# Memory scores over 40 key columns without a mask, with the spread moved into the normalisation

## The chip, the cores and the metric

The kernel runs on one core of a Trainium2 chip. The metric is the device time of one execution in microseconds (us); lower is better. A profile is one execution taken by the hardware profiler; its span runs from the first to the last instruction. Engines: PE is the matmul side of TensorE and PEld its weight loads, DVE is VectorE, ACT is ScalarE, POOL is GpSimd, SP is SyncE, which here issues DMAs.

## The reference

A layer of recurrent-memory attention followed by a squared-ReLU feed-forward block, on 2048 tokens of width 640, with 32 heads of 128 columns, 8 memory rows and segments of 32 tokens. The 64 segments depend on each other through the memory:

```python
idx = jnp.arange(L)                       # L = M + seg_len = 40
mask = (idx[:, None] < M) | (idx[:, None] >= idx[None, :])
mem = mem0
for s in range(n_seg):                    # 64 segments
    h = jnp.concatenate([mem, layernorm(x)[segment s]], axis=1)
    q, k, v = h @ Wq, h @ Wk, h @ Wv      # per head
    scores = where(mask, q @ k.T * Dh ** -0.5, -1e9)
    o = (softmax(scores) @ v) @ Wo
    mem = o[:, :M]                        # the next segment's memory
    outs.append(o[:, M:])
h = x + concatenate(outs)
out = h + relu(layernorm(h) @ w1 + b1) ** 2 @ w2 + b2
```

The mask lets the 8 memory queries see all 40 keys; token queries see the memory and the tokens up to their own.

## The kernel before

**Steps.** `step(b, sp)` is one segment s = 4b + sp (`NS` = 64 of them, in blocks of four). The matrix products of one row block are split over the four column groups of TensorE, so that four matmuls with 32 weight columns run at a time ("a round"). Of the 32 rows that a step projects itself, 8 are memory and 24 (`HD`) are tokens; the last 8 tokens of a segment (`TL`), the tail, are projected ahead for four segments at once (`tail_units`) and copied into place by `tails_in` (L320): queries to `qT` columns 32 to 39, keys to `kT`. `NK` = 40, `SEG` = 32.

**Memory queries.** The 8 memory queries of the 32 heads are worked on apart from the token queries, since only they are needed for the next step's memory. Heads come in two halves (n = 0, 1), four column groups g and four places j. `spread` (L369) copies the memory queries of head p into `qz[:, p, 8j:8j+8]`, with zeros elsewhere, so that four heads (j = 0 to 3) can accumulate into one 32-row block of PSUM, each in its own 8 rows. `scores(n)` (L413) makes 16 such matmuls at L421; before them, four matmuls at L416 put `bmask` into columns 32 to 63. The tail's 8 keys lie four times in `kT`, in columns 32 + 8j + k, and `bmask` is 0 where the column's j is the row's own and -1e9 elsewhere. `soft1(n)` (L425) takes the maximum (L427, DVE) and the exponential with its row sum (L430, ACT); `soft2(n)` (L434) the reciprocal (L436), the scaling to probabilities (L438) and a transpose of 32x32 blocks (L440), all on DVE. The copy in place j is what lets `values(n)` (L443) use the tail's values of four heads, stacked over (j, k) in `vt4`, in one matmul of 32 rows (L454), behind 16 for the other keys (L449).

**Token queries.** `token_scores` (L486) has a mask round at L489 and matmuls over 40 columns at L493; their softmax (L527 to L552) goes on beside the output product, and their values (`token_values`, L348) are made a step later. There the spread to four places is made with `same`, a 0/1 pattern (128 x 4 x 8) that is 1 where j is the row's own place: GpSimd multiplies the transposed tail probabilities by it at L572.

**Order.** All engines' queues are in the order of the program text; nothing is reordered by a scheduler. In a step TensorE has: query and key projections (L206), `scores(0)`, part of the value projection, `token_scores(0)`, more of the value projection, `scores(1)`, `token_scores(1)`, `token_values` of the step before (L355, L360), `values(0)`, the rest of the value projection, the output product (L238) with `values(1)` inside it, filling work (`fill`: tail projections and the tails' output products), and `mem_to_hT` (L312), which sets the new memory rows in the next step's input. The last step has no memory queries, so there are 63 x 2 calls of `scores`. `sm`, `pw` and `pm` share one PSUM buffer (`chn`, one buffer), so each waits until the one before has been read.

Of the kernel before, what the change touches and what calls it, by code (L numbers as in the profile page):

```python
# [8 lines left out]
ACT = mybir.ActivationFunctionType  # L9
ALU = mybir.AluOpType  # L10
AX = mybir.AxisListType
F32 = mybir.dt.float32
BF16 = mybir.dt.bfloat16
# [3 lines left out]
def kernel(  # L17
# [16 lines left out]
    nc = tc.nc  # L34
    _, S, D = A_x.shape
    _, H, E = A_Wq.shape
    M = A_mem0.shape[1]
    SEG = 32
    G = 4
# [8 lines left out]
    TL = SEG - HD  # L48
    NK = SEG + M
# [4 lines left out]
    scale = float(E) ** -0.5  # L54
    EPS = 1e-5
    NEG = -1.0e9
# [4 lines left out]
    const = ctx.enter_context(tc.tile_pool(name="const", bufs=1))  # L61
# [7 lines left out]
    s2 = ctx.enter_context(tc.tile_pool(name="s2", bufs=2))  # L69
# [8 lines left out]
    ident = const.tile([128, 128], BF16)  # L78
# [7 lines left out]
    nc.vector.memset(mask[:], 0.0)  # L86
    nc.gpsimd.affine_select(out=mask[0:32], in_=mask[0:32], compare_op=ALU.is_ge, fill=NEG, base=0,
                            pattern=[[0, HG], [-1, SEG]], channel_multiplier=1)
    bmask = const.tile([128, 4, TL], BF16)
    qz = const.tile([128, H, 32], BF16)  # L90
    nc.vector.memset(qz[:], 0.0)
    qzf = qz[:].rearrange("p h r -> p (h r)")
# [1 line left out]
    same = const.tile([128, 4, TL], BF16)  # L94
# [2 lines left out]
        nc.vector.tensor_copy(out=same[r], in_=ident[r, r].rearrange("p (j k) -> p j k", k=TL))  # L97
    nc.vector.tensor_reduce(out=diag[:], in_=same[:], op=ALU.add, axis=AX.X)
    nc.vector.tensor_copy(out=same[:], in_=diag[:].unsqueeze(2).to_broadcast([128, 4, TL]))
    nc.vector.tensor_scalar(out=bmask[:], in0=same[:], scalar1=-1.0, scalar2=-NEG, op0=ALU.add, op1=ALU.mult)  # L100
    qT = const.tile([128, H, NK], BF16)
    kT = const.tile([128, H, 2 * SEG], BF16)
    oT = const.tile([128, H, NK], BF16)
    nc.vector.memset(oT[:], 0.0)
    oTts = [const.tile([128, H, 32], BF16, name="oTt%d" % k) for k in range(2)]
# [30 lines left out]
    for ch in range(2):  # L136
        nc.scalar.dma_start(out=o0[32 * ch:32 * ch + M, :].rearrange("m (c f) -> m c f", f=64),
                            in_=A_mem0[0].rearrange("m (c t f) -> t m c f", t=2, f=64)[ch])
# [181 lines left out]
    def tails_in(b, sp, which="qk", h0=0, h1=H):  # L320
        q, k = [tails[b][w][:].rearrange("p h (k s) -> p h s k", s=4)[:, h0:h1, sp, :] if w in which else None for w in "qk"]
        if "q" in which:
            nc.gpsimd.tensor_copy(out=qT[:, h0:h1, SEG:NK], in_=q)
        if "k" in which:
            nc.gpsimd.tensor_copy(out=kT[:, h0:h1, SEG:2 * SEG].rearrange("p h (j k) -> p h j k", k=TL),  # L325
                                  in_=k.unsqueeze(2).to_broadcast([128, h1 - h0, 4, TL]))

    vt4s, stores = {}, []
    vt_d = dram.tile([NB, 4, 128, 2 * E], BF16)
# [50 lines left out]
    def step(b, sp, v=None):  # L380
# [30 lines left out]
        sms, ems, zms = {}, {}, {}  # L411

        def scores(n):  # L413
            sm = chn.tile([128, 512], F32, tag="ch", name="sm")
            for g in range(G):
                nc.tensor.matmul(sm[32 * g:32 * g + 32, SEG:2 * SEG], lhsT=ident[:, 0:32],  # L416
                                 rhs=bmask[:].rearrange("p j k -> p (j k)"), start=True, stop=False, skip_group_check=True)
            for j in range(4):
                for g in range(G):
                    p = n * 16 + g * 4 + j  # L420
                    nc.tensor.matmul(sm[32 * g:32 * g + 32, 0:2 * SEG], lhsT=qz[:, p, :], rhs=kT[:, p, :],  # L421
                                     start=False, stop=(j == 3), skip_group_check=True)
            sms[n] = sm

        def soft1(n):  # L425
            mx = s2.tile([128, 1], F32, tag="mx", name="mx")
            nc.vector.tensor_reduce(out=mx[:], in_=sms[n][:, 0:2 * SEG], op=ALU.max, axis=AX.X, negate=True)  # L427
            em = s2.tile([128, 2 * SEG], BF16, tag="em", name="em")
            zm = s2.tile([128, 1], F32, tag="zm", name="zm")
            nc.scalar.activation(out=em[:], in_=sms[n][:, 0:2 * SEG], func=ACT.Exp, bias=mx[:, 0:1], scale=1.0,  # L430
                                 accum_out=zm[:])
            ems[n], zms[n] = em, zm

        def soft2(n):  # L434
            rm = s2.tile([128, 1], F32, tag="rm", name="rm")
            nc.vector.reciprocal(out=rm[:], in_=zms[n][:])  # L436
            pm = s2.tile([128, 2 * SEG], BF16, tag="pmem", name="pmem")
            nc.vector.tensor_scalar(out=pm[:], in0=ems[n][:], scalar1=rm[:, 0:1], scalar2=None, op0=ALU.mult)  # L438
            pT = s2.tile([128, 2 * SEG], BF16, tag="pTm", name="pTm")
            nc.vector.transpose(out=pT[:], in_=pm[:])  # L440
            return pT
# [31 lines left out]
        def first_half():  # L473
            if not last:
                scores(0)
                soft1(0)
# [26 lines left out]
        if not last:  # L503
            pT0 = soft2(0)
# [3 lines left out]
        if not last:  # L508
            scores(1)
        token_scores(1)  # L510
        if not last:
            soft1(1)
# [11 lines left out]
        if not last:  # L524
            pT1 = soft2(1)
# [8 lines left out]
        if not last:  # L534
# [14 lines left out]
                                op=ALU.mult)  # L549
        pk = s1.tile([128, HG, 32], BF16, tag="pk", name="pk")  # L550
        nc.gpsimd.tensor_tensor(out=pk[:], in0=ek[:, :, 0:SEG], in1=rk[:].unsqueeze(2).to_broadcast([128, HG, SEG]),
                                op=ALU.mult)  # L552
# [9 lines left out]
        if not last:  # L562
            run(fill, 4 if outs else 6)
            mem_to_hT(o, hT4s[(s + 1) // 4], (s + 1) % 4)
            tails_in((s + 1) // 4, (s + 1) % 4)
# [5 lines left out]
        for u in range(2):  # L571
            nc.gpsimd.tensor_tensor(out=pTx[:, u], in0=pTt[:, u, HD:32].unsqueeze(1).to_broadcast([128, 4, TL]),  # L572
                                    in1=same[:], op=ALU.mult)
# [95 lines left out]
    def start():  # L669
# [5 lines left out]
        def stream(which, w, dst):  # L675
            pa = pop.tile([128, 4, 512], F32, tag="po", name="pa")
            for c in range(DC):
                for n in range(2):
                    proj(w, "half" if which == "v" else "columns", main, n, pa[:, n, :], c, c + 1)
                for n in range(2):  # L680
                    proj(w, "order" if which == "v" else "columns", lambda c: tail_rows(0, c), n, pa[:, 2 + n, :], c, c + 1)
                if c < DC - 1:
                    run(units, DC)
            for n in range(2):
                if which == "v":
                    nc.scalar.copy(out=v[:, n * 512:(n + 1) * 512], in_=pa[:, n, :])
                else:
                    row = rowtile()[:]
                    evac_row(which, row, pa[:, n, :])
                    flip(row, dst, n)  # L690
                    tail_out(0, which, n, pa[:, 2 + n, :])
                    run(late, 100)
                    tails_in(0, 0, which, n * 16, (n + 1) * 16)
            if which == "v":
                for n in range(2):
                    tail_out(0, which, n, pa[:, 2 + n, :])
# [110 lines left out]
    for t in range(S // NT):  # L807
# [6 lines left out]
        for fc in range(FC):  # L814
            ps = mmtile()
            for c in range(DC):
                if fc < FFULL:
                    nc.tensor.matmul(ps[:], lhsT=w1[:, c, fc * 128:(fc + 1) * 128], rhs=hnT[:, c, :],  # L818
                                     start=(c == 0), stop=(c == DC - 1))
                    continue  # L820
                for hh in range(2):
                    nc.tensor.matmul(ps[FREM * hh:FREM * (hh + 1), 0:HT], lhsT=w1[:, c, fc * 128:F],
                                     rhs=hnT[:, c, HT * hh:HT * (hh + 1)], start=(c == 0), stop=(c == DC - 1))
# [4 lines left out]
            if more and fc >= 1 and (fc - 1) // 3 < NK4:  # L828
                k, stage = divmod(fc - 1, 3)
# [10 lines left out]
        for q in range(NK4):  # L840
# [6 lines left out]
            for hh in range(2):  # L847
                k = pr + 2 * hh
                for fc in range(FFULL):
                    nc.tensor.matmul(y[:, hh, 0:DH], lhsT=f1T[:, fc, k * 128:(k + 1) * 128], rhs=w2[:, fc, cs],  # L850
                                     start=(fc == 0), stop=False, skip_group_check=True)
                if more and q and (hh == 0 or q == 1):
                    k = q if hh == 0 and q > 1 else hh
                    prep_pe(t + 1, k, hn_[k])()
            for hh in range(2):
                r = slice(FREM * hh, FREM * (hh + 1))
                nc.tensor.matmul(y[:, hh, 0:DH], lhsT=f1T[r, FFULL, pr * 128:(pr + 1) * 128], rhs=w2[r, FFULL, cs],
                                 start=False, stop=True, skip_group_check=True)
# [40 lines left out]
```

## Time and profile before

| | |
|---|---|
| time, median of 3 runs | 1029.64 us (1028.8 to 1029.67) |
| profiled execution, span | 1025.5 us (the profile gives this execution no other time of its own; the runs lie 3.3 to 4.2 us above the span) |
| granted TensorE clock, mean | 0.997 |
| PE busy | 971.4 us |
| PEld busy | 576.6 us |
| DVE busy | 619.0 us |
| ACT busy | 533.2 us |
| POOL busy | 309.1 us |
| stretch of the steps in full flow, 62 to 878 us | PE busy 790.0, DVE 528.8, ACT 457.9, POOL 262.1 of 816 us |

Busy time is the union of an engine's instructions. In rows of groups, the line is that of the program, then engine, operation, output<-inputs, shapes and count; behind the bar the busy us and the mean ns of one instruction, then the idle time of the engine just before them and what ended it. In rows of the timeline the start and the length in us come first. Matmuls overlap in the array, so the length of one (some 0.18 us for the shortest) is not what it costs when others follow.

### The profile page before, as it was taken

The page shows a single profiled execution, that of the slowest core. Times are in us where ns is not written, and L with a number is a line of the kernel's source. Part 1 is how long each engine was busy: PE and PEld are TensorE (multiplying, and loading weights), DVE is VectorE, ACT ScalarE, POOL GpSimd, SP SyncE. Part 2 cuts the span into 40 slices and gives each one's busy share as a digit, 9 for nine tenths or more (in the row PEclk, how much of TensorE's full clock was granted, in tenths as well). Part 3 has the DMA queues.
Part 4 walks back from the last instruction along what each step waited for, and adds up shares of the span by engine and source line. Part 5 has one row for each costly group of instructions (what it writes and reads, how often), then busy time and mean ns, then how long its engine had stood idle before and what let it go on. Part 6 is the DMA issues. An engine that isn't in the chain of part 4 may idle for free.

```text
span 1025.5 us, 58960 instructions
## 1 busy us (share of the span) xinstructions
PE 971.4 (95%) x26951; PEld 576.6 (56%) x26960; DVE 619.0 (60%) x1740; ACT 533.2 (52%) x1229; POOL 309.1 (30%) x803
## 2 busy tenths in 40 slices
PE   5789999999999999999999999999999999999998
PEld 2345555655655555555655665555566565555565
DVE  2246666766666757666666666666666676466432
ACT  3335554555555555555555555555555555533431
POOL 1123333333333333333333332323232333443210
PEclk9989999999999999999999999999999999999999
DMA  9950101000101010001000000000000110612200
GB/s 367 397 180 21 23 7 30 7 25 6 35 7 31 6 40 8 26 11 31 11 25 11 26 16 20 17 15 27 14 22 8 47 34 7 204 55 65 77 26 26
DMA packets 39112, 51.57 MB, mean 50 GB/s; under 512 B 5968, under 2 KB 35024, under 8 KB 36944
## 3 DMA queue, kind: packets, MB, share of 16 engines
q1 hardware_dynamic: 38080, 47.48, 13.9%
q8 instruction: 210, 3.44, 1.4%
q10 hardware_dynamic: 784, 0.34, 0.1%
q14 instruction: 38, 0.31, 0.1%
HBM read 38.37 MB, written 9.44 MB: 47 GB/s over the span
## 4 chain that ended last, share of the span: by engine, by line
PE 87%; DMA 6%; DVE 2%; issue 2%; ACT 1%; SPq 1%; ACTq 0%; DVEq 0%; POOL 0%; POOLq 0%
PE ps L206 48%; PE pw L238 15%; PE y L850 5%; PE ps L818 4%; PE ps L238 3%; PE po L449 2%; PE po L355 2%; PE sm L421 2%; DMA wq<-in_B_w_dram 1%; DMA vt_d<-row 1%; PE ps L493 1%; DMA wv<-in_A_Wv_dram 1%; DMA wo<-in_A_Wo_dram 1%; PE pm L316 1%; DMA vt<-vt_d 1%
## 5 line engine op out<-in xcount | busy, mean ns | idle before, releaser
L206 PEld LDWEIGHTS <-hT 128*32 128x32 bf16 x7680 | 195.4, 97 | 179.6 <-issue 17.9
L238 PE MATMUL pw<-wo,oT 128*32 128x320 bf16 x4224 | 185.6, 300 | 7.6 <-issue 5.6
L206 PE MATMUL ps<-wv,hT 128*32 128x512 bf16 x2520 | 171.5, 379 | 2.3 <-issue 1.6
L206 PE MATMUL ps<-wq,hT 128*32 128x512 bf16 x2520 | 160.0, 382 | 5.3 <-DVE hT L318 5.3
L206 PE MATMUL ps<-wk,hT 128*32 128x512 bf16 x2520 | 159.3, 381 | 0.1
L238 PEld LDWEIGHTS <-oT 128*32 128x32 bf16 x4224 | 106.7, 96 | 59.8 <-issue 13.0
L222 ACT ACTIVATE row<-ps 128x512 bf16<-128x512 f32 x156 | 93.3, 599 | 75.5 <-PE ps L206 75.5
L227 DVE STREAM_TRANSPOSE qT<-row 128x512 bf16<-128x512 bf16 x128 | 90.3, 705 | 66.0 <-ACT row L222 65.9
L548 POOL TENSOR_TENSOR pkt<-ek,rk 128x64 bf16<-128x64 bf16 x64 | 18.8, 294 | 360.6 <-DVE rk L546 360.6
L224 ACT CAST row<-ps 128x512 bf16<-128x512 f32 x115 | 67.9, 591 | 33.1 <-PE ps L206 31.4
L325 POOL COPY kT<-kTt 128x1024 bf16<-128x1024 bf16 (+1 forms) x65 | 71.8, 1105 | 11.7 <-DVE kTt L227 11.7
L374 POOL COPY qz<-qT 128x96 bf16<-128x96 bf16 x126 | 33.4, 265 | 139.1 <-DVE qT L227 138.9
L206 PEld LDWEIGHTS <-hTt 128*32 128x32 bf16 x1920 | 53.6, 97 | 31.5 <-issue 1.3
L245 ACT COPY otmp<-pw 64x320 f32<-64x320 f32 x66 | 27.9, 422 | 81.3 <-PE pw L238 81.3
L365 ACT CAST oT<-po 128x512 bf16<-128x512 f32 x128 | 68.7, 589 | 1.6
L246 DVE TENSOR_TENSOR o<-pw,otmp 64x320 bf16<-64x320 f32 x66 | 31.8, 482 | 61.3 <-ACT otmp L245 61.3
L523 ACT CAST v<-ps 128x512 bf16<-128x512 f32 x63 | 36.9, 585 | 59.0 <-PE ps L206 59.0
L227 DVE STREAM_TRANSPOSE kT<-row 128x512 bf16<-128x512 bf16 x65 | 46.1, 709 | 31.1 <-ACT row L224 31.1
L544 DVE TENSOR_REDUCE zk<-ek 128x8 f32<-128x320 bf16 x64 | 31.1, 486 | 51.1 <-ACT ek L542 51.1
L850 PE MATMUL y<-wq,wk 128*128 128x320 bf16 x416 | 61.2, 299 | 0.4 <-DVE wk L827 0.4
L405 ACT CAST row<-ps 128x256 bf16<-128x256 f32 x126 | 40.7, 375 | 30.5 <-PE ps L206 29.9
L502 ACT CAST v<-ps 128x512 bf16<-128x512 f32 x63 | 36.9, 585 | 30.5 <-PE ps L206 30.5
(113 smaller groups left out, 1629.5 us busy)
## 6 DMA issues: line engine op xcount, KB each, us to landing
wv<-in_A_Wv_dram SPq DMA_DIRECT2D x5, 1024.0 KB
wq<-in_A_Wq_dram SPq DMA_DIRECT2D x5, 1024.0 KB
wk<-in_A_Wk_dram SPq DMA_DIRECT2D x5, 1024.0 KB
vt<-vt_d SPq DMA_DIRECT2D x60, 64.0 KB
xt<-in_A_x_dram SPq DMA_DIRECT2D x20, 160.0 KB
vt_d<-row SPq DMA_DIRECT2D x22, 128.0 KB
wo<-in_A_Wo_dram SPq DMA_DIRECT2D x2, 1280.0 KB
wo<-in_A_Wo_dram SPq DMA_DIRECT2D x4, 640.0 KB
```

The costliest lines, as they stand in the source:

```text
L206: nc.tensor.matmul(ps[32 * k:32 * k + 32, :], lhsT=lhs(c), rhs=wr[:, c, n, k], start=(c == 0), stop=(c == DC - 1))
L222: nc.scalar.mul(out=row, in_=ps, mul=scale)
L224: nc.scalar.copy(out=row, in_=ps)
L227: nc.vector.transpose(out=dst[:, n * 16:(n + 1) * 16, 0:32], in_=row.rearrange("p (h e) -> p h e", e=32))
L238: nc.tensor.matmul(pw[32 * j:32 * j + 32, 0:DH], lhsT=lhs(p), rhs=wov2[:, head(p), ch], start=(h == 0), stop=(h == 15))
L325: nc.gpsimd.tensor_copy(out=kT[:, h0:h1, SEG:2 * SEG].rearrange("p h (j k) -> p h j k", k=TL), in_=k.unsqueeze(2).to_broadcast([128, h1 - ...
L365: nc.scalar.copy(out=oTg[:, n, :, :, M:NK], in_=po[:, :, n * 128:(n + 1) * 128].rearrange("p g (j q) -> p g j q", q=32))
L405: nc.scalar.copy(out=row[:, u * 256:(u + 1) * 256], in_=ps[:, u * 256:(u + 1) * 256])
L502: nc.scalar.copy(out=v[:, 0:512], in_=ps0[:])
L523: nc.scalar.copy(out=v[:, 512:1024], in_=ps1[:])
L818: nc.tensor.matmul(ps[:], lhsT=w1[:, c, fc * 128:(fc + 1) * 128], rhs=hnT[:, c, :], start=(c == 0), stop=(c == DC - 1))
L850: nc.tensor.matmul(y[:, hh, 0:DH], lhsT=f1T[:, fc, k * 128:(k + 1) * 128], rhs=w2[:, fc, cs], start=(fc == 0), stop=False, skip_group_chec ...
```

## The change

The tail's keys are kept once: `kT` has 40 columns a head instead of 64, and the copy at L325 writes 8 columns a head instead of 32. `bmask` and the four matmuls with it are gone; the first matmul of each column group starts the accumulation. The maximum and the exponential go over 40 columns. In `soft2`, the 32 first columns are scaled as before, and the 8 tail columns are multiplied by the reciprocal and by `same`, read four times by a broadcast, which writes the same 64 columns of `pm` as before. The transpose and `values` are unchanged.

```diff
-    bmask = const.tile([128, 4, TL], BF16)
...
-    nc.vector.tensor_scalar(out=bmask[:], in0=same[:], scalar1=-1.0, scalar2=-NEG, op0=ALU.add, op1=ALU.mult)
     qT = const.tile([128, H, NK], BF16)
-    kT = const.tile([128, H, 2 * SEG], BF16)
+    kT = const.tile([128, H, NK], BF16)
...
         if "k" in which:
-            nc.gpsimd.tensor_copy(out=kT[:, h0:h1, SEG:2 * SEG].rearrange("p h (j k) -> p h j k", k=TL),
-                                  in_=k.unsqueeze(2).to_broadcast([128, h1 - h0, 4, TL]))
+            nc.gpsimd.tensor_copy(out=kT[:, h0:h1, SEG:NK], in_=k)
...
             sm = chn.tile([128, 512], F32, tag="ch", name="sm")
-            for g in range(G):
-                nc.tensor.matmul(sm[32 * g:32 * g + 32, SEG:2 * SEG], lhsT=ident[:, 0:32],
-                                 rhs=bmask[:].rearrange("p j k -> p (j k)"), start=True, stop=False, skip_group_check=True)
             for j in range(4):
                 for g in range(G):
                     p = n * 16 + g * 4 + j
-                    nc.tensor.matmul(sm[32 * g:32 * g + 32, 0:2 * SEG], lhsT=qz[:, p, :], rhs=kT[:, p, :],
-                                     start=False, stop=(j == 3), skip_group_check=True)
+                    nc.tensor.matmul(sm[32 * g:32 * g + 32, 0:NK], lhsT=qz[:, p, :], rhs=kT[:, p, :],
+                                     start=(j == 0), stop=(j == 3), skip_group_check=True)
...
-            nc.vector.tensor_reduce(out=mx[:], in_=sms[n][:, 0:2 * SEG], op=ALU.max, axis=AX.X, negate=True)
-            em = s2.tile([128, 2 * SEG], BF16, tag="em", name="em")
+            nc.vector.tensor_reduce(out=mx[:], in_=sms[n][:, 0:NK], op=ALU.max, axis=AX.X, negate=True)
+            em = s2.tile([128, NK], BF16, tag="em", name="em")
...
-            nc.scalar.activation(out=em[:], in_=sms[n][:, 0:2 * SEG], func=ACT.Exp, bias=mx[:, 0:1], scale=1.0,
+            nc.scalar.activation(out=em[:], in_=sms[n][:, 0:NK], func=ACT.Exp, bias=mx[:, 0:1], scale=1.0,
...
-            nc.vector.tensor_scalar(out=pm[:], in0=ems[n][:], scalar1=rm[:, 0:1], scalar2=None, op0=ALU.mult)
+            nc.vector.tensor_scalar(out=pm[:, 0:SEG], in0=ems[n][:, 0:SEG], scalar1=rm[:, 0:1], scalar2=None, op0=ALU.mult)
+            nc.vector.scalar_tensor_tensor(out=pm[:, SEG:2 * SEG].rearrange("p (j k) -> p j k", k=TL),
+                                           in0=ems[n][:, SEG:NK].unsqueeze(1).to_broadcast([128, 4, TL]),
+                                           scalar=rm[:, 0:1], in1=same[:], op0=ALU.mult, op1=ALU.mult)
```

## The prediction

> **What bounds the kernel now.** I read the page first: busy time of the engines, then the chain that ended last.
>
> ```profile
> span 1025.5 us, 58960 instructions
> ...
> PE 971.4 (95%) x26951; PEld 576.6 (56%) x26960; DVE 619.0 (60%) x1740; ACT 533.2 (52%) x1229; POOL 309.1 (30%) x803
> ...
> PE 87%; DMA 6%; DVE 2%; issue 2%; ACT 1%; SPq 1%; ACTq 0%; DVEq 0%; POOL 0%; POOLq 0%
> ```
>
> TensorE is busy for 95% of the span and carries 87% of the chain; the other engines idle 40% or more. But a matmul's recorded time includes its pipeline, so busy time cannot price a short one. The timeline can: what counts is the time from the start of one line's first matmul to the start of the next line's.
>
> ```profile
> 303.29 0.19 PE L416 MATMUL sm<-bmask,ident 128*32 128x32 bf16 x4
> 303.31 0.29 PE L421 MATMUL sm<-kT,qz 128*32 128x64 bf16 x16
> 303.43 0.39 PE L206 MATMUL ps<-wv,hT 128*32 128x512 bf16 x4
> ...
> 303.86 0.28 PE L489 MATMUL ps<-mask,ident 128*32 128x256 bf16 x4
> 303.97 0.27 PE L493 MATMUL ps<-kT,qT 128*32 128x40 bf16 x16
> 304.07 0.39 PE L206 MATMUL ps<-wv,hT 128*32 128x512 bf16 x4
> ```
>
> The mask round (L416) holds the array from 303.29 to 303.31, the scores (L421, 64 columns) to 303.43. Right behind them lie the same sixteen products at 40 columns: L493, the segment tokens' scores, from 303.97 to 304.07. In the unrounded starts of the trace the medians over all calls are 28 ns for L416, 113 ns for L421 and 104 ns for L493 where no change of tile shape follows. All around, the array streams without a gap: L206 starts the moment L421 is in.
>
> Third, the waits of TensorE (engine, line, releaser: us in total, times, longest):
>
> ```profile
> PEld L206 <- issue: 19.2, 38, 2.0
> PEld L449 <- ACT v L523: 15.6, 57, 0.7
> PEld L238 <- issue: 14.2, 29, 1.6
> PEld L449 <- issue: 8.5, 20, 0.9
> PE sm L421 <- POOL kT L325: 1.7, 1, 1.7
> PE sm L416 <- ACT em L430: 0.6, 1, 0.6
> ```
>
> No wait for the softmax of the memory queries appears beyond single cases. "Issue" is time for which the profile has no releaser. In the starts of the trace, between 62 us and 878 us, fifty breaks of 0.05 to 0.87 us, 21.5 us together, all fall after the same count of TensorE instructions: every 256 (weight loads and matmuls counted together), always behind the run of short products L421 to L454. They come where 256 instructions went by in under about 2.8 us; blocks that took over 3.4 us have none. TensorE then waits for its own instructions.
>
> **The change part by part.** The span is 1025.5 us and the median of the runs 1029.64, so 4.1 us lie around the span; I subtract from the median.
>
> *Mask matmuls gone, 64 columns to 40.* Two score calls in each of 63 steps. Step 0 runs at 48 to 54 us, before TensorE waits for the output weights (the DMA wo that ends at 59.2 us in the chain), so its two count nothing: 124 calls. Each saves 28 + (113 - 104) = 37 ns of the array: 124 x 0.037 = 4.6 us. Every later wait in a step (DVE oT L213, DVE o L246, DVE hT L318) starts from a TensorE instruction behind the scores, so it moves along and gives nothing back.
>
> The narrowing is worth only 9 of these 37 ns. The Trainium skill (TensorEngine Tiling, section Instruction Overhead) says that a matmul carries some 60 cycles of overhead, so that one column costs as much as 60; by it the sum would be little more than the mask's, 124 x 0.028 = 3.5 us. The rows agree in kind: 28 ns for a round of four at 32 or at 64 columns, 26 at 40.
>
> *Fewer TensorE instructions.* 124 x 8 = 992 of 49,832 in that stretch go. Least: the breaks shrink with the count, 2% of 21.5 = 0.4 us. Most: the block that ends in a break usually contains scores(1); without its 8 quick mask instructions it takes in one more 512-column round (0.216 us) for the mask's 0.028, so each break shrinks by 0.19: 50 x 0.19 = 9.4 us. With instructions of average spacing (816 us / 49,832 = 16.4 ns, so 8 x 0.0164 - 0.028 = 0.10) it is 5 us; but the 256 grid also moves against the steps and makes some breaks anew. I take 2 us. The Trainium skill (Runtime: NRT & Kernel Launch, section Instruction fetch mechanics) says that instructions come in blocks of 256 and that the crossing is mostly hidden; by that this term is 0 and the sum 4.6 us. The trace has the 256 but not the hiding: 50 breaks, 0.43 us on average.
>
> *VectorE: one more instruction per softmax.* Nearest rows:
>
> ```profile
> L438 DVE TENSOR_SCALAR pmem<-em,rm 128x64 bf16<-128x64 bf16 x126 | 30.5, 242 | 4.5
> L427 DVE TENSOR_REDUCE mx<-sm 128x1 f32<-128x64 f32 x126 | 28.0, 222 | 17.3 <-PE sm L421 17.2
> L529 DVE TENSOR_TENSOR tk<-ps,mxk 128x320 f32<-128x320 f32 x64 | 31.5, 492 | 2.2
> L100 DVE TENSOR_SCALAR bmask<-same 128x32 bf16<-128x32 bf16 x1 | 0.2, 174 | 0.0
> ```
>
> The new product of probabilities and pattern (32 elements, a broadcast operand, a per-row scalar) lies between 174 ns (L100, 32 elements) and 492 (L529, 320 elements with a broadcast). It is nearest to L438: 240 ns. Plus some 40 ns to the next instruction, less 30 on the scaling, now 32 wide (242 towards 174): 0.25 us. The maximum and the exponential over 24 fewer columns give back perhaps 20 ns each. On VectorE that is 126 x 0.2 = some 25 us of 406 idle ones. What covers it: from the end of the transpose L440 to the first weight load of L449 the trace has a median of 507 ns for the first half (least 343) and 470 for the second (least 356). A VectorE result reaches a weight load some 60 ns after its end (L213 to L238 at 306.55 to 306.60), so 0.45 and 0.41 us are free; from the first go 38 ns more, as its softmax starts 37 ns earlier but its values stand 75 ns earlier in TensorE's stream. At 0.25 nothing waits. Behind it in VectorE's queue are L213 (waits for TensorE, 0.5 us idle before it), mxk and tk (L527, L529). tk ends 100 to 150 ns before ScalarE's exponential L542, which will so start some 0.1 us later; its results go on to L548 and L551 on GpSimd and back to L569, none asked for by TensorE before the next step. Cost: 0.
>
> *GpSimd's copy of the keys.* L325 falls from 128x1024 (1120 ns) to the form of L323, 128x256 (461 ns). GpSimd idles 70% and its waits are for others: 0. The one wait of 1.7 us for it is in step 0, ahead of the output weights: 0. The mask's set-up (L100, 0.2 us) lies under the first loads: 0. The 80-byte rows of kT are those that qT has today, and flips into both cost the same (705 and 709 ns): 0.
>
> *The wait that L416 carried.* The mask matmul waits for ScalarE (em of the first half, which frees the scores' buffer). Now L421 inherits it, which already waits for GpSimd in its weight load and for VectorE in its matmul. A third releaser may need an instruction of its own on TensorE's queue, as elsewhere:
>
> ```profile
> L206 PEldq EVENT_SEMAPHORE  x2: 51/51/51, 21.5 to 34.7; - x2
> L493 PEldq EVENT_SEMAPHORE  x1: 51/51/51, 880.8 to 880.8; - x1
> ```
>
> Behind 512-column rounds (L206) it cost nothing: the next round came 215 ns later as always. At 880.84, behind a 256-column round, the next came 83 ns late, though the keys it waited for were finished only at 880.80. Bounds: 0 to 0.083 x 62 = 5.1 us. scores(1) stands behind 512-column rounds: I take 0. Queued behind it is all of TensorE, but em is done 0.7 us earlier.
>
> Sum: 4.6 + 2 = 6.6 us; 1029.64 - 6.6 = 1023.0.
>
> **The rivals.**
> *Only the array's time is won*, the breaks do not shrink (or move so as to cancel): 1029.64 - 4.6 = 1025.0. For it: which blocks break depends on where the grid falls. Still faster. With the forecast: 0.78, of which a third here.
> *The new wait eats it.* The separate semaphore instruction costs its upper bound: 1029.64 - 4.6 + 5.1 = 1030.1; half of it with the breaks unchanged gives 1027.6. For it: the 83 ns at 880.84; against: the two at L206. No change: 0.10.
> *VectorE becomes late.* It decides from a new product of about 0.40 us (0.41 + 0.03 - 0.04) on. At L529's 0.49: values(1) waits 0.49 + 0.04 - 0.03 - 0.41 = 0.09 us, and values(0), with 0.04 back from the maximum and the exponential, 0.46 + 0.04 - 0.45 = 0.05; over 62 steps 8.7 us: 1029.64 - 4.6 + 8.7 = 1033.7. Against: L438 and L100 are half as long. Slower: 0.12, with all that makes VectorE late by more.
>
> **How the numbers follow.** About 0.2% (2.1 us) is what a measurement here can tell from no change, so faster means below 1027.6. The predicted time is the forecast's, 1023.0. The range goes down to 1019.5 (4.6 plus the 5 us that average spacing gives, and a little) and up to 1028.5, into the case of the new wait; slower than before, and the worse half of "same", are left out. Chances: faster 0.78, same 0.10, slower 0.12.
>
> **What would show it.** Right: no L416; L421's successor (now the stream's next line) starts some 0.10 us after L421's first matmul instead of 0.14 after L416's; issue waits of L206, L238 and L449 below 41.9 us together; L325 near 461 ns; the new VectorE line near 240 ns; PE's waits for L440 still absent. Wrong: a row "L449 <- DVE" of several us (VectorE late), or EVENT_SEMAPHOREs at L421 with a matmul cadence over 216 ns in front of scores(1).

## The result and the profile after

The changed kernel took 1026.75 us (median of 5 runs, 1023.47 to 1027.17) against 1029.67 for the kernel before: ratio 0.9963, 95% interval 0.9947 to 0.9979. Run again later (e_after, below) the ratio was 0.9981 (0.9966 to 0.9996). The mean of the two, 0.9972, is 2.9 us. The runs listed with a span of their own lie some 2.1 us above it, so the profiled execution of the kernel before (span 1025.5 us) was one of about 1027.6 us, and the two profiles are less far apart (0.8 us of span) than the medians. The page of the changed kernel, its total, busy times and chain:

```profile
span 1024.7 us, 58138 instructions
...
PE 967.2 (94%) x26447; PEld 571.1 (56%) x26456; DVE 636.3 (62%) x1865; ACT 533.9 (52%) x1229; POOL 265.0 (26%) x803
...
PE 89%; DMA 5%; issue 2%; DVE 2%; ACT 1%; SPq 1%; ACTq 0%; DVEq 0%; POOL 0%; POOLq 0%
```

504 matmuls fewer, 17 us more on VectorE, 44 us less on GpSimd; TensorE sets the end as before. (The lines of the program moved up: L206 is L204 now, L238 L236, L421 L415, L449 L446; the maximum, L427 before, is L421 now, and the transpose L440 is L437. In the experiments they shift again by a few.) The timeline around the two score calls of one step:

```profile
302.64 0.61 PE L204 MATMUL ps<-wk,hT 128*32 128x512 bf16 x8
303.07 0.27 PE L415 MATMUL sm<-kT,qz 128*32 128x40 bf16 x16
303.17 0.60 PE L204 MATMUL ps<-wv,hT 128*32 128x512 bf16 x8
...
304.89 0.27 PE L415 MATMUL sm<-kT,qz 128*32 128x40 bf16 x16
304.99 0.30 PE L490 MATMUL ps<-kT,qT 128*32 128x40 bf16 x16
```

From the first score product to what follows it is 0.10 us, where mask and scores had taken 0.14. In unrounded starts the median is 104 ns against 28 + 113: the 37 ns of the prediction, to the nanosecond. The first half starts where the projection leaves off, and so does the second, although a wait instruction now stands in front of it (a row of the changed kernel's line L415, and of the keys' copy L323):

```profile
L415 PEldq EVENT_SEMAPHORE  x61: 51/51/51, 69.6 to 852.0; - x61
...
L323 POOL COPY kT<-kTt x65: 295/427/520, 49.4 to 874.1; 128x256 bf16<-128x256 bf16 x63, 128x128 bf16<-128x128 bf16 x2
```

The median from the last 512-column matmul to the first score product is 204 ns in the second half, where all 61 stand; in the kernel before it was 205 to the mask round: the wait lies under the projection's stream. VectorE's groups (count, then busy us and mean ns):

```profile
L526 DVE TENSOR_TENSOR tk<-ps,mxk 128x320 f32<-128x320 f32 x64 | 31.5, 492 | 2.2
L433 DVE SCALAR_TENSOR_TENSOR pmem<-em,rm,same 128x32 bf16<-128x32 bf16 x126 | 31.0, 246 | 0.0
L432 DVE TENSOR_SCALAR pmem<-em,rm 128x32 bf16<-128x32 bf16 x126 | 29.5, 235 | 4.5
L421 DVE TENSOR_REDUCE mx<-sm 128x1 f32<-128x40 f32 x126 | 23.4, 186 | 4.5 <-PE sm L415 2.9
```

The new product takes 246 ns (240 forecast). The waits of TensorE, however, hardly moved:

```profile
PEld L204 <- issue: 18.4, 34, 1.9
PEld L236 <- issue: 15.6, 27, 2.1
PEld L446 <- ACT v L520: 15.1, 56, 0.6
PEld L446 <- issue: 8.3, 20, 0.8
PEld L415 <- POOL qz L371: 1.8, 1, 1.8
```

The three issue rows that the prediction summed to 41.9 us give 42.3. The breaks, added up in the trace's starts from step 5 on, are 22.0 us before and 21.1 after, fifty in both. All fall on boundaries of 256 TensorE instructions, where the 61 semaphore waits count with the weight loads and matmuls; most boundaries show none (183 lie in that stretch before). These sums hold to a few us only, since they depend on what spacing is taken as the usual one. Step by step they are others: one step lost 0.9 us of them, another gained 1.15.

The two profiled executions, compared at the moment when the last memory is written (near 875 us), are 2.5 us apart: the first step ends 0.8 us later (the DMA of the output weights ends at 60.0 us instead of 59.2), and the steps behind it are 3.3 us shorter; breaks, bias wait (below) and TensorE's clock change that by about 0.1. The median step is 66 ns shorter, where two calls save 74. Behind that moment 1.7 of the 2.5 us are lost: in the stretch from 880 to 895 us the granted clock is 0.89 after and 1.00 before. That is not the change's doing: from 60 to 70 us it is 0.83 after and 0.66 before, 6.8 us of halved clock in both executions, at other places; and in the second profile of the changed kernel (e_after) all 6.8 us lie at 60 us, as before.

### The profile page after: what moved, and what is told of

It reads as the page before. It is cut to its first block, busy times and chain, and to the rows that moved or that the text cites. A ratio compares the mean times of both kernels' runs of the same rounds, so it can differ in the third digit from the quotient of the medians.

```text
span 1024.7 us, 58138 instructions
## 1 busy us (share of the span) xinstructions
PE 967.2 (94%) x26447; PEld 571.1 (56%) x26456; DVE 636.3 (62%) x1865; ACT 533.9 (52%) x1229; POOL 265.0 (26%) x803
## 4 chain that ended last, share of the span: by engine, by line
PE 89%; DMA 5%; issue 2%; DVE 2%; ACT 1%; SPq 1%; ACTq 0%; DVEq 0%; POOL 0%; POOLq 0%
PE ps L204 48%; PE pw L236 16%; PE y L847 5%; PE ps L815 5%; PE ps L236 4%; PE po L446 2%; PE po L352 2%; PE ps L490 1%; DMA vt_d<-row 1%; DMA wv<-in_A_Wv_dram 1%; PE sm L415 1%; DMA wo<-in_A_Wo_dram 1%; PE pm L314 1%; DMA vt<-vt_d 1%; PE ps L486 1%
## 5 line engine op out<-in xcount | busy, mean ns | idle before, releaser
L204 PEld LDWEIGHTS <-hT 128*32 128x32 bf16 x7680 | 196.2, 96 | 178.9 <-issue 17.0
L236 PE MATMUL pw<-wo,oT 128*32 128x320 bf16 x4224 | 187.1, 302 | 9.3 <-issue 5.6
L204 PE MATMUL ps<-wv,hT 128*32 128x512 bf16 x2520 | 172.5, 379 | 2.4 <-issue 1.6
L204 PE MATMUL ps<-wq,hT 128*32 128x512 bf16 x2520 | 159.2, 381 | 5.3 <-DVE hT L316 5.3
L204 PE MATMUL ps<-wk,hT 128*32 128x512 bf16 x2520 | 159.4, 381 | 0.1
L236 PEld LDWEIGHTS <-oT 128*32 128x32 bf16 x4224 | 106.2, 97 | 63.0 <-issue 15.0
L204 PEld LDWEIGHTS <-hTt 128*32 128x32 bf16 x1920 | 53.0, 97 | 32.3 <-issue 1.3
L823 ACT ACTIVATE wv<-ps,b1f 128x512 bf16<-128x512 f32 (+1 forms) x56 | 37.6, 672 | 27.1 <-PE ps L815 26.7
```

Of the source, the lines that this page charges most:

```text
L204: nc.tensor.matmul(ps[32 * k:32 * k + 32, :], lhsT=lhs(c), rhs=wr[:, c, n, k], start=(c == 0), stop=(c == DC - 1))
L236: nc.tensor.matmul(pw[32 * j:32 * j + 32, 0:DH], lhsT=lhs(p), rhs=wov2[:, head(p), ch], start=(h == 0), stop=(h == 15))
L823: nc.scalar.activation(out=r[:, 0:w], in_=ps[:, 0:w], func=ACT.Relu, bias=b1f[:, fc:fc + 1], scale=1.0)
```

## Experiments

Theories: **A**, the gain is the array's 37 ns a call and the breaks stay; **B**, the breaks are a shortage of instructions, so that time in the array without instructions is partly free and instructions cost more than their array time; **C**, a break depends on which instructions stand at the 256 boundary.

**Time without instructions (e_wide).** Of the changed kernel:

```diff
-                    nc.tensor.matmul(sm[32 * g:32 * g + 32, 0:NK], lhsT=qz[:, p, :], rhs=kT[:, p, :],
+                    nc.tensor.matmul(sm[32 * g:32 * g + 32, 0:3 * NK].rearrange("p (a k) -> p a k", k=NK), lhsT=qz[:, p, :],
+                                     rhs=kT[:, p, :].unsqueeze(1).to_broadcast([128, 3, NK]),
```

> The changed kernel, its score products streaming 120 columns instead of 40 (the same 40 key columns three times, of which only the first 40 results are read); no instruction is added. A round of four takes 120/40 of the stream: some 52 ns instead of 26, so 4 x 26 x 124 = 13 us more in TensorE's array. Theory A (only the array's time counts, the breaks behind every 256 TensorE instructions stay as they are, 21 to 22 us together): 1026.75 + 13 = 1039.8. Theory B (a break is what 256 instructions lack to some 2.8 us, as the prediction's upper bounds had it): the block that ends in a break holds the second score call, so it lasts 0.1 us longer and each of 50 breaks shrinks by as much: 1026.75 + 13 - 5 = 1034.8, breaks 17 us together.

Measured: 1025.24 us, ratio to the kernel before 0.9981 (0.9967 to 0.9994). The stream is as long as was meant: 210 ns a call instead of 104 from start to start, 13 us in 124 calls. A row of its line (the length of one matmul), then its waits:

```profile
L415 PE MATMUL sm<-kT,qz x2016: 212/216/227, 49.5 to 868.4; 128*32 128x120 bf16 x184
```

```profile
PEld L204 <- issue: 18.2, 41, 2.0
PEld L236 <- issue: 11.4, 22, 1.9
PEld L447 <- issue: 6.0, 19, 0.6
```

Breaks from step 5 on: 11.9 us, against 21.1 and 25.1 in two profiles of the changed kernel. 13 us of added stream cost 1 +- 2 us of time (0.9981 against 0.9972), because 9 to 13 us of breaks went. Theory A (1039.8) falls. B has the direction, but its number fails too: it gave 1034.8 us and 17 us of breaks. The run also bears on the narrowing to 40 columns: with three times the columns, 69 ns a call more array time than the kernel before, the kernel is still no slower than that one. If 106 ns a call cost some 1 us, the 9 ns that the narrowing saves are an estimated 0.1 us; no run has the narrowing alone.

**Instructions with the same time (e_rounds4).** Of the changed kernel:

```diff
+            for u in range(4):
+                for g in range(G):
+                    nc.tensor.matmul(sm[32 * g:32 * g + 32, 0:NK], lhsT=ident[:, 0:32], rhs=zt[:],
+                                     start=(u == 0), stop=False, skip_group_check=True)
```

`zt` is a tile of zeros; the score products behind these rounds no longer start the accumulation.

> The changed kernel with four rounds (16 matmuls, 16 weight loads) of zeros over 40 columns ahead of each score call: nearly the same array time as 120 columns, 4 x 26 ns x 124 = 12.9 us, but 32 TensorE instructions more a call. Theory A: 1026.75 + 12.9 = 1039.7, breaks 21 to 22 us. Theory B: the block that ends in a break loses 32 instructions of average spacing (0.525 us) for 0.104, so each of 50 breaks grows by 0.42: breaks 43 us, 1060. Theory C (a break depends on where the 256 boundary falls: it is seen when it falls in the run of short products, some 250 instructions a step; their number grows by 32 in front of those): breaks 22 x 282/250 = 25 us, 1042.5.

Measured: 1059.79 us, ratio 1.0312 (1.0291 to 1.0333). Its timeline at a first half, then its waits:

```profile
312.14 0.28 PE L416 MATMUL sm<-zt,ident 128*32 128x40 bf16 x16
312.25 0.32 PE L421 MATMUL sm<-kT,qz 128*32 128x40 bf16 x16
312.40 0.41 PE L206 MATMUL ps<-wv,hT 128*32 128x512 bf16 x4
```

```profile
PEld L206 <- issue: 22.5, 29, 2.8
PEld L238 <- issue: 16.2, 30, 1.0
PEld L452 <- issue: 14.5, 24, 1.2
```

The added rounds take 0.11 us a call, as the wide stream did; the time grows by 35 us (1.0312 against 0.9972), not by 1. Breaks are 37.5 us, 62 of them. Of the 35 us, 13 are the array's and 12 to 16 breaks; the other 6 to 10 sit in smaller delays that I did not take apart (in the first half the score products behind the rounds take 0.15 us instead of 0.10). A gave 1039.7 and C 1042.5, and both fall. B gave 1060 and alone is near, but in part by luck: it expected 43 us of breaks, and the delays that it did not have make up for those that are missing. An added instruction in the dense part of the step costs some 35 us / 4032 = 8.7 ns here, 2.7 times its array time (13 us / 4032 = 3.2).

**What a break waits for.** The DMA records of the traces tell. The queue q8 brings instructions in packets of 16 KB; its rows before and after (packets, MB, share of the 16 DMA engines' span):

```profile
q8 instruction: 210, 3.44, 1.4%
```

```profile
q8 instruction: 207, 3.39, 1.4%
```

That is one packet for every boundary of 256 TensorE instructions, in number: 210 and 210 before, 207 and 207 after, 222 and 222 in e_rounds4, and the same in all fourteen traces. Counted in order, no block from step 5 on has its first instruction sooner than 1.19 us after its own packet ended. Of 616 breaks of 0.15 us or more, 604 end 1.2 to 1.6 us after it. (The other twelve are 0.2 us at a 512-column round, whose usual spacing is that long.) An example from the trace before: the packet ran from 304.74 to 306.09 us, TensorE stopped at 306.74 and went on at 307.37. So a break is a wait for the next block of instructions, the shortage that B assumes. B's fixed 2.8 us for a block is too simple: the packets start at times that scatter by more than a microsecond against the boundary before, and with them the size of a break.

**VectorE's cover (e_spread3).** Of the changed kernel: the new product runs three times (`for _ in range(3):` ahead of it).

> The changed kernel with the new VectorE product done three times in a row (the same result written again). One took 246 ns in the profile, and delayed the transpose behind it by 149 ns in the second half and by 225 in the first, against the kernel before; two more therefore delay it by 0.3 to 0.45 us. From the end of the transpose to the first weight load of the values the changed kernel has 321 ns left (second half) and 282 (first), of which some 60 are the way from VectorE to TensorE. So the cover is 0.26 and 0.22 us. Prediction's reading (cover as measured): late by 0.04 to 0.2 us in 124 halves: 5 to 25 us more. Theory B adds that a wait in front of the values gives time to the instruction supply, so breaks shrink by as much as half of it: 3 to 12 us. If the cover were larger than it looks: 0.

Measured: 1039.84 us, ratio 1.0096 (1.0074 to 1.0118): 12.8 us over the changed kernel (0.9972). Its two rows of TensorE's waits in front of the values (weight load, matmul), and the product's group:

```profile
PEld L447 <- issue: 28.4, 116, 0.8
PE po L447 <- DVE pTm L438: 19.8, 108, 0.6
```

```profile
L434 DVE SCALAR_TENSOR_TENSOR pmem<-em,rm,same 128x32 bf16<-128x32 bf16 x378 | 94.5, 250 | 8.9
```

The cover ends where it was read: TensorE now stops in front of the values in both halves of nearly every step (116 cases, against 19 to 24 in the kernels above; the weight load's row says issue, but the matmul's names VectorE's transpose, and the median from its end to the first matmul is 53 ns in both halves, where the changed kernel has 291 and 326). In the trace's starts these stops add 29 us, 0.25 us a half, a little over the upper expectation, and the breaks fall from 21 to 25 us down to 6.8. 29 less 14 to 18 is 11 to 15 us, and 12.8 were measured. So a wait in the step pays for part of itself: the next instructions arrive meanwhile.

**Where the boundaries fall (six runs, and the changed kernel once more, e_after).** Small matmuls at the very start, while TensorE waits for its first rows, move all later boundaries; in the changed kernel and in the kernel before, with n = 32, 64, 96:

```diff
+    pad = mmtile()
+    for k in range(n):
+        nc.tensor.matmul(pad[32 * (k % 4):32 * (k % 4) + 32, 0:8], lhsT=ident[:, 0:32], rhs=ident[:, 0:8], start=True, stop=True)
     ln_stats(0)
```

> The changed kernel with 64 small matmuls (128 TensorE instructions with their weight loads) at the very start, while TensorE waits for the first rows: the 256 boundaries fall half a block elsewhere in every step, all else is as it was. All theories: the single breaks land in other steps; their sum, if the prediction's reading of a lottery holds, stays within 22 +- 3 us, and the time within 1026.75 +- 3. A sum outside that would say that the changed kernel's place in the grid was a lucky or unlucky one, and that the term of 2 us in the prediction could not be seen for that reason.

> The changed kernel as it is, once more, on the same chip as the three below. Its own profile tells how far the breaks of one program differ between executions. If theory B (TensorE is short of instructions: 256 of them take at least some 2.8 us) is right, the breaks are made anew in each execution: their sum again 17 to 22 us, and the ratio to the kernel before again 0.9963 +- 0.0016. If the 21 us of the first profile were fixed by the program, the sum is 21 again.

> The kernel before, with the 64 small matmuls at the start that the changed kernel had in e_shift128 (there: ratio 0.9925, breaks 17 us instead of 21). Lottery of the grid: a shift of half a block moves the breaks to other steps and their sum by some us either way; expected 20 +- 3 us and a ratio of 0.998 +- 0.003. If the shift helps both kernels alike (some other effect of the early matmuls): ratio 0.996. If the kernel before had been in an unlucky place and the change merely moved it: breaks 17, ratio 0.995, and half of the change's gain would be place and not work.

> The changed kernel with 32 small matmuls (64 TensorE instructions) at the start: a third of four places of the 256 boundaries (0, 64, 128, 192). So far the breaks of the changed kernel are 21.1, 25.1 (the same program again) and 18.6 us (its late-bias form) at place 0, 17.3 and 16.5 at place 128; of the kernel before 22.0 and 22.7. Theory A (breaks do not shrink on the average over places): means over the four places equal, some 21 us, and the changed kernel faster by the array's 4.6 us on the average. Theory B (fewer instructions, smaller breaks; from e_rounds4, where 32 instructions and 104 ns more a call gave 16 us more of breaks, 8 instructions and 28 ns less should give 4 us less, and the 9 ns of the narrowing take back 0.8): mean of the changed kernel 3.3 us under that of the one before, times on the average 8 us apart. For this run: A 21 +- 4 us of breaks, B 18.5 +- 4.

> The changed kernel with 96 small matmuls (192 TensorE instructions) at the start: the fourth place. A: breaks 21 +- 4 us, ratio 0.996 +- 0.004; B: 18.5 +- 4, ratio 0.993 +- 0.004. It counts in the mean only.

> The kernel before with 64 TensorE instructions more at the start. Breaks 22 +- 4 us and a ratio of 1.000 +- 0.004 by either theory; it counts in the mean of the kernel before over four places.

> The kernel before with 192 TensorE instructions more at the start, the last of eight. Breaks 22 +- 4 us, ratio 1.000 +- 0.004. Means of times over the four places, changed against before: A 4.6 us apart, B 8 us.

Measured, ratio to the kernel before (on the same chip) with its interval, and breaks from step 5 on in one profile each:

| instructions ahead | before: ratio | breaks, us | changed: ratio | breaks, us |
|---|---|---|---|---|
| 0 | 1 | 22.0 | 0.9963 (0.9947 to 0.9979), 0.9981 (0.9966 to 0.9996) | 21.1, 25.1 |
| 64 | 0.9983 (0.9968 to 0.9998) | 19.6 | 0.9943 (0.9927 to 0.9959) | 21.4 |
| 128 | 1.0032 (1.0020 to 1.0045) | 22.7 | 0.9925 (0.9902 to 0.9948) | 17.3 |
| 192 | 1.0021 (1.0005 to 1.0037) | 23.3 | 0.9961 (0.9946 to 0.9977) | 23.8 |
| mean (place 0 counted once) | 1.0009 | 21.9 | 0.9950 | 21.4 |

Work that nobody waits for moves either kernel by up to 5 us. That this is the place of the boundaries is argued: at 128 the same early matmuls move the two kernels opposite ways, which an effect common to both would not do. At a given place the change is worth between 2.9 us (place 0, where it was measured first) and 11 us (place 128). The means differ by 0.0059 +- 0.0011 (the intervals' half widths added in quadrature), 6.1 +- 1.1 us: a little more than the array's 4.6, less than the 8 of theory B's estimate. The breaks themselves do not decide it: their means differ by 0.5 us, and two profiles of the same program by 4. So the total gain over four places is shown, and B is shown for large additions (e_wide, e_rounds4, e_spread3). How the change's own gain splits into array time and breaks stays open: if array time counts in full, breaks have between nothing and some 2.6 us of it, and after e_wide it need not count in full.

**GpSimd's queue (e_bias_late).** The changed kernel's wait of 1.8 us for GpSimd, seen in its timeline at step 4, and two rows of the same place in the kernel before:

```profile
107.67 0.20 POOL L589 CAST b1f<-b1b 128x14 f32<-128x14 bf16 x1 [3.83 <-DMA b1b<-in_B_b_dram]
107.81 0.27 POOL L371 COPY qz<-qT 128x96 bf16<-128x96 bf16 x1
...
108.13 0.25 PEld L415 LDWEIGHTS <-qz 128*32 128x32 bf16 x16 [1.76 <-POOL qz L371]
```

```profile
106.55 0.20 POOL L592 CAST b1f<-b1b 128x14 f32<-128x14 bf16 x1 [2.47 <-DMA b1b<-in_B_b_dram]
...
107.00 0.25 PEld L421 LDWEIGHTS <-qz 128*32 128x32 bf16 x16 [0.86 <-POOL qz L374]
```

A cast for the feed-forward part waits for its DMA at the head of GpSimd's queue, the spread of the queries stands behind it, and TensorE behind that; in the kernel before the same chain cost 0.9 us. The edit takes the cast out of `ffn_biases` and issues it four steps later:

```diff
-        nc.gpsimd.tensor_copy(out=b1f[:], in_=b1b[:])
...
                 ffn_biases()
+            if (b, sp) == (2, 0):
+                nc.gpsimd.tensor_copy(out=b1f[:], in_=b1b[:])
```

> The changed kernel with GpSimd's cast of the feed-forward bias (b1f) moved from the step after its DMA is issued to four steps later. In the profile the cast waits 3.8 us for its DMA at the head of GpSimd's queue, the spread of the queries stands behind it, and TensorE waits for that at its score products (1.3 us on PE, 1.8 on PEld). If that wait is real it goes: 1026.75 - 1.5 = 1025.3, and no row of the score products waiting for GpSimd is left but that of the first step. If TensorE would have waited there for something else: 1026.75.

Measured: ratio 0.9932 (0.9905 to 0.9959). The row is gone. Against the changed kernel's 0.9963 and 0.9981 that is 3 and 5 us, over the 1.5 expected, but its profile also drew few breaks (18.6 us), and the intervals touch or nearly so: the wait is shown, the size beyond 1.5 us is not.

**Both (e_shift_bias).** The changed kernel with 64 matmuls ahead and the late cast.

> The changed kernel with both: the 64 small matmuls at the start and the late cast of the bias. If the two effects are apart (place of the boundaries; GpSimd's queue in one step), they add: 0.9963 x (0.9925 / 0.9963) less 1.5 us = 0.991, 1018.3 us where the kernel before takes 1027.5. If both only drew other breaks: 0.993 +- 0.002.

Measured: 1019.36 us, ratio 0.9902 (0.9877 to 0.9927), the fastest of all twelve and clear of both kernels, though not of e_shift128 (0.9925), which lacks the late cast alone. Expected 0.991; its breaks are 16.5 us. Part of this is a drawn place and would be lost with the next edit of TensorE's program; the late cast would stay.

## Why the prediction was right or wrong

The direction and the range held; the 1023.0 us was 3.75 under the first measurement. The direction held narrowly. By the prediction's own line for faster, 1027.6 us, the first measurement's 1026.75 is faster, while the ratio of the second measurement, 0.9981, comes to 1027.7, just over it. At place 0 the gain is less than half of the 6.6 us forecast and lies below the first rival's too (4.6 us, 1025.0). That the mean over four places, 6.1 us, comes close to 6.6 owes something to luck, since the two terms that make it up were each misread in part. One of the signs of being right did not come: the issue waits were to fall below 41.9 us, and they are 42.3, and 48.8 in e_after.

*Mask and width, 4.6 us:* right in size as array time (37 ns a call seen). As to time it was read too simply: the prediction took array time as time, and e_wide shows that 13 us of it can be nearly free. The sum by the Trainium skill (TensorEngine Tiling, Instruction Overhead), 3.5 us for the mask round alone, leaves out what e_wide shows to be worth little, the narrowing's 9 ns of array time without an instruction less. Its rule of equal cost up to 60 columns agrees with rounds of 28 ns at 32 and 64 columns and 26 at 40; at 120 columns a round takes 52.

*Fewer instructions, 2 us:* the mechanism, a wait for instructions, was right; the size was not seen. 992 instructions went in the 124 calls and 61 semaphore waits came, so 931 fewer were to be fetched. At the place where the boundaries lay the breaks are 22.0 us before, 21.1 and 25.1 in two profiles after: no fall that both show. Over four places the excess of the gain over the array's is 1.5 +- 1.1 us, which holds the 2 if array time counts in full. What failed was to give a term of this kind one value: another place of the boundaries makes 5 us. The statement of the Trainium skill (Runtime: NRT & Kernel Launch, Instruction fetch mechanics) that crossing a block of 256 is mostly hidden holds for the count of the crossings and not for their time: 50 of 183 show a break in the kernel before, where the prediction saw no hiding at all, but the ten programs that differ in places and in the late cast alone, the change aside, have 16 to 25 us of breaks each.

*VectorE, 0:* right. One product of 246 ns, cover left over, and the cover's end found by e_spread3. One step of the working named the wrong instruction: the transposed probabilities are read by the matmul, not by its weight load, which waits for the values. The two stood 4 to 10 ns apart, so the cover was the same.

*GpSimd's copy, 0:* right (1120 to 427 ns, and 44 us less busy, with nobody waiting). *The inherited wait, 0:* right; 61 semaphore instructions appeared and cost nothing. Its rival, and VectorE's, are refuted in the changed kernel.

*Not in the prediction:* the wait behind the bias cast: its 0.9 us is in the waits of the kernel before and was passed over; it grew to 1.8 us as its DMA landed later. And the spread between executions: the changed kernel ran from 1023.5 to 1027.2 us in its first five runs.

## What to carry to other kernels

Where dense runs of short matmuls leave TensorE waiting with no releaser, count instructions before array time: here each weight load or matmul added cost 2.7 times its array time (e_rounds4), and columns added without instructions were nearly free (e_wide). Set the instruction packets in the DMA records beside the breaks: they tell whether TensorE waits for its program. Before judging a change of a few us in such a kernel, move the boundaries with some idle early matmuls and compare means over places. And read every wait that occurs once: a cast waiting for a DMA at the head of GpSimd's queue stopped TensorE.

## What the runs showed of the hardware

- Breaks fall on boundaries of 256 TensorE instructions, 0.4 us on average, at 50 of 183 of them in the kernel before, in programs of 52,900 to 56,900 TensorE instructions; they shrink when the same instructions take longer (e_wide 11.9 us, e_spread3 6.8) and grow with more of them (e_rounds4 37.5). A break ends 1.2 to 1.6 us after the DMA of the next 16 KB of instructions does (604 of 616 breaks in fourteen traces), so it can end with no DMA under way.
- On VectorE, 32 elements cost what 64 did: 235 and 242 ns for the scaling, 246 for the product with two tensors; but the product adds only 149 ns to the chain from the scaling's start to the transpose's (275 ns before, 424 after), since it starts 144 ns after the scaling, before that ends.
